# When an expert's second matrix gets its scale: after the first block of the first layer, or after the second

## The chip, the cores and the metric

The kernel runs on one core of one Trainium2 chip. The metric is the time of one execution in microseconds on the device; a kernel is run several times and the median is quoted. All times inside an execution are microseconds from its first instruction.

## The reference, cut to what matters

Three layers follow each other on 4 x 576 positions of width 512. The first is a retention layer with 8 heads. The second routes each position to one of 8 experts, and it is the one that the change touches:

```python
e = fresh_e if s == 0 or local_gate[b, s] < 0.5 else prev_e   # which expert
h = np.maximum(x[b, s] @ w1[e], 0.0)        # 512 -> 1024, "first layer"
out[b, s] = p[e] * (h @ w2[e])              # 1024 -> 512, "second layer"
```

The third layer is a Fourier mixing over positions and channels, a normalisation and a dense network of width 2048 with a residual (`u + relu(un @ w_ch1) @ w_ch2`). Everything is float32 in the reference.

## The kernel before, in words

**Split arithmetic.** Every float32 matrix is turned into two fp16 matrices, a high part `wh` and a residue `wl`, with one power-of-two scale for each matrix. A product is then three groups of fp16 matmuls (high x high, residue x high, high x residue). To get there a matrix of an expert goes through these steps (class `Weights`), in four pieces of 128 x 1024:

- `load`: SP issues the DMA of a piece into a tile `wst`.
- `absmax` (L234): ScalarE (ACT) sums magnitudes of a piece.
- `peak` (L243 to L255): three small VectorE (DVE) instructions reduce these to one exponent for each partition and write it on a diagonal, the tile `diag`.
- `spread` (L257 to L261): TensorE (PE) multiplies `diag` by a matrix of ones, so that every partition sees all exponents (L260), and DVE takes the maximum (`wg`, L261).
- `scale` (L263 to L269): two small DVE instructions make the scale `ws`.
- `split`: for each piece ACT writes the high part `wh` (`high`, L276), then DVE the residue `wl` (`low`, L281).

**The passes.** The function `moe` runs over eight lists of positions, `e` = 0 to 7; we call them passes 0 to 7. `CAPS` sets their widths: 128, 416, 320, 320, 320, 288, 288, and 128 (the rest of the last list is done later). A pass is a first layer and a second layer. The first layer is eight blocks; a block is 12 matmuls (L807) into one PSUM bank of the pool `p1`, which has four banks. Each block's result is taken out by `relu`: ACT writes the high part of `hid` (L823), DVE its residue (L825); only then is the bank free, and block 4 needs the bank of block 0, block 5 that of block 1, and so on. The second layer (L837) runs in tiles of 128 positions; ACT scales the result out (L849) and POOL scatters it to DRAM.

**Work beside the matmuls.** While a pass runs on the current expert's first matrix, its second matrix is split, and the next expert's matrices are measured and loaded. Besides, the third layer's weights, which arrive as 64-bit numbers (`raw`), are converted by DVE: `conv.first` (three instructions, L294 to L298) and `conv.second` (L303, L306), stored by SP, and measured by ACT (`conv.absmax`).

**What sets the order.** The order is written out by hand. The table `SLOTS` has one dict for the first layers (n = 2e) and one for the second layers (n = 2e + 1). A step's number k puts it behind block int(k) of a first layer (or behind the corresponding tile of a second layer); within one place lower numbers come first, and a negative number means the head of place 0. The function `halves` (L924) turns the table into a list for each place, and `moe` emits for each block `f`: the block's matmuls, the steps of place `f`, then the block's `relu`:

```python
products(nc, ps, *w.dst, xt, f)
for do in todo[f]:
    do()
```

So each engine gets its instructions in that order and works through them in that order; a step that waits holds up whatever stands behind it on its own engine. SP's queue holds, per pass, loads of `raw` and stores of converted weights, one big transposing DMA that brings the next pass's positions (`xt`, L1012), small ones, and eight loads of pieces. Another `spread` stands in the middle of each second layer's first tile (the argument `amid`), for the next expert's first matrix; it is not touched.

Of the kernel before, what the change touches and what calls it, by code (L numbers as in the profile page):

```python
# [863 lines left out]
class Late:  # L864
# [18 lines left out]
    def outputs(self, bank):  # L883
# [11 lines left out]
    dict(  # L895
        own=-1,
        second=0,
        spread=1,
        split=(1.1, 1.2, 2.1, 3.1),
        raw=1.2,  # L900
        store=1.3,
        fetch=1.4,
# [6 lines left out]
        spread=-1,  # L909
        first=(0, 4.2),  # L910
        factors=0.2,
        split=(0.5, 0.6, 1.5, 2.7),
# [1415 lines left out]
```

## Time and profile before

| what | value |
|---|---|
| time before, median of 3 runs | 814.44 us (811.02 to 817.1) |
| the profiled execution's own time | 811.84 us |
| its span, first to last instruction | 810.1 us |
| mean granted TensorE clock | 0.982 |
| PE busy | 740.1 us, 91% of the span |
| DVE busy | 593.3 us, 73% |
| ACT busy | 412.3 us, 51% |
| first layers of passes 2 to 7 | between 191.5 and 349.5 us |

The page is one profiled execution. "Busy" is a sum over the whole span; which engine limits a stretch has to be read in that stretch, from the waits. A row of the timeline gives the start, the length, the engine, the line, the operation, and in brackets how long the engine had been idle before and which instruction released it. In rows the names carry no buffer numbers: `ps` is a PSUM bank, `peak` the bank of a `spread`, `wst` a loaded piece, `d` a converted piece.

### The profile page before, as it was taken

The numbers are of one execution on the slowest core, as the hardware profiler recorded it, in microseconds if no ns is written. First come the engines' busy times: TensorE is split into PE (matmuls) and PEld (weight loads), VectorE is DVE, ScalarE is ACT, GpSimd is POOL, SyncE is SP. The second block draws the span as 40 slices with busy tenths as digits, with TensorE's granted clock in tenths as the row PEclk, the third lists the DMA queues.
The fourth block names the chain that finished last, engine by engine and source line by source line (L and its number), as shares of the span: only waits on it lengthen the run. The fifth ranks groups of instructions, "written<-read, shape, count | busy, mean of one in ns | idle before, by whom it ended". The sixth has DMA issues, their size and how long they took to land. (4 is left out here: it accounts for less than half of the span.)

```text
span 810.1 us, 17225 instructions
## 1 busy us (share of the span) xinstructions
PE 740.1 (91%) x6571; PEld 552.6 (68%) x6571; DVE 593.3 (73%) x1432; ACT 412.3 (51%) x829; POOL 129.9 (16%) x225
## 2 busy tenths in 40 slices
PE   7889888898889988889998999979899999999996
PEld 5778675555455555567644546868788888888885
DVE  3667886886879879757787976977958495737362
ACT  1445655675977977844764644605523361504040
POOL 3555543102012102111100002010010101010101
PEclk9999999899999999999999999999999999999998
DMA  9987439999998998843165457630270016100000
GB/s 287 357 292 263 162 112 291 236 312 367 263 378 289 262 352 296 265 135 110 46 213 185 154 188 199 198 75 15 92 217 2 27 53 170 53 34 21 27 2 27
DMA packets 91931, 142.29 MB, mean 176 GB/s; under 512 B 48117, under 2 KB 49018, under 8 KB 90815
## 3 DMA queue, kind: packets, MB, share of 16 engines
q1 hardware_dynamic: 87246, 126.78, 50.0%
q0 software_dynamic: 4592, 14.31, 4.6%
q8 instruction: 54, 0.88, 0.5%
q14 instruction: 39, 0.31, 0.1%
HBM read 97.55 MB, written 35.12 MB: 164 GB/s over the span
## 5 line engine op out<-in xcount | busy, mean ns | idle before, releaser
L1628 PE MATMUL g<-gxt,wh 128*128 128x256 f16 (+1 forms) x992 | 142.9, 284 | 3.0 <-DMA gxt<-un 2.9
L1942 PEld LDWEIGHTS <-hd 128*128 128x128 f16 x1176 | 114.2, 98 | 26.8 <-issue 7.2
L1628 PEld LDWEIGHTS <-wh 128*128 128x128 f16 x1056 | 103.0, 98 | 28.4 <-issue 6.7
L281 DVE SCALAR_TENSOR_TENSOR wl<-wst,ws,wh 128x1024 f16<-128x1024 f32 (+1 forms) x82 | 100.1, 1254 | 18.0 <-ACT wh L276 17.7
L276 ACT ACTIVATE wh<-wst,ws 128x1024 f16<-128x1024 f32 x80 | 88.6, 1139 | 39.1 <-DVE ws L269 39.1
L807 PE MATMUL ps<-xt,wh 128*128 128x320 f16 (+4 forms) x544 | 82.4, 290 | 21.3 <-DVE hid L825 13.8
L807 PEld LDWEIGHTS <-wh 128*128 128x128 f16 x640 | 58.9, 102 | 45.0 <-issue 27.3
L837 PE MATMUL ps<-wh,hid 128*128 128x512 f16 (+2 forms) x528 | 84.4, 302 | 0.8 <-ACT wh L276 0.8
L1942 PE MATMUL g<-wh,hd 128*128 128x256 f16 x448 | 78.3, 273 | 4.2 <-DVE u L1971 2.0
L1802 POOL DMA_INDIRECT out<-u,orow x18 | 19.3, 1075 | 388.8 <-DVE u L1971 291.6
L1628 PE MATMUL g<-gxt,wl 128*128 128x256 f16 (+1 forms) x496 | 79.5, 283 | 0.0
L837 PEld LDWEIGHTS <-hid 128*128 128x128 f16 (+2 forms) x792 | 46.4, 100 | 44.0 <-issue 3.6
L1913 DVE SCALAR_TENSOR_TENSOR s<-g,r 128x256 f32<-128x256 f32 x168 | 53.3, 374 | 30.3 <-ACT hd L1907 29.7
L234 ACT ACTIVATE wh<-wst 128x1024 bf16<-128x1024 f32 x66 | 69.1, 1048 | 3.8 <-DVE wst L306 3.8
L1971 DVE SCALAR_TENSOR_TENSOR u<-g,ffs,u 128x256 f32<-128x256 f32 (+1 forms) x63 | 34.1, 568 | 49.3 <-PE g L1942 48.7
L1906 ACT ACTIVATE r<-g 128x256 f32<-128x256 f32 x56 | 21.2, 378 | 91.4 <-PE g L1628 85.4
L851 POOL DMA_INDIRECT x<-y,mt x25 | 32.3, 1291 | 206.1 <-ACT y L849 159.4
L1886 ACT ACTIVATE hd<-s 128x640 f16<-128x640 f32 x56 | 41.3, 737 | 47.1 <-DVE s L1913 47.1
L1942 PE MATMUL g<-e,hd 128*128 128x256 f16 x504 | 60.0, 273 | 5.0 <-DVE u L1971 4.0
L1942 PE MATMUL g<-wl,hd 128*128 128x256 f16 x224 | 61.0, 272 | 0.0
L1628 PEld LDWEIGHTS <-wl 128*128 128x128 f16 x528 | 51.7, 98 | 11.4 <-issue 0.6
L837 PE MATMUL ps<-wl,hid 128*128 128x512 f16 (+2 forms) x264 | 56.3, 301 | 0.7 <-DVE wl L281 0.7
(302 smaller groups left out, 1304.6 us busy)
## 6 DMA issues: line engine op xcount, KB each, us to landing
wst<-in_moe_w SPq DMA_DIRECT2D x64, 512.0 KB
raw<-in_ch SPq DMA_DIRECT2D x14, 1024.0 KB
qk<-in_qkv SPq DMA_DIRECT2D x18, 512.0 KB
vk<-in_qkv SPq DMA_DIRECT2D x16, 512.0 KB
pair<-ch SPq DMA_DIRECT2D x32, 256.0 KB
ch<-d SPq DMA_DIRECT2D x14, 512.0 KB
wst<-ch SPq DMA_DIRECT2D x14, 512.0 KB
u<-u SPq DMA_DIRECT2D x9, 512.0 KB
```

The costliest lines, as they stand in the source:

```text
L234: self.nc.scalar.activation(out=x, in_=t, func=ACTF.Abs, accum_out=self.am[:, j : j + 1])
L276: self.nc.scalar.activation(out=self.dst[0][:, j, :], in_=self.pieces[j], func=ACTF.Copy, scale=self.by(j))
L281: self.nc.vector.scalar_tensor_tensor(out=l[:, j, c], in0=self.pieces[j][:, c], scalar=self.by(j), in1=h[:, j, c], op0=ALU.mult, op1=ALU.s ...
L807: nc.tensor.matmul(out=ps, lhsT=m[:, k, 128 * f : 128 * f + 128], rhs=xt[:, x + k, :], start=(k == 0 and i == 0), stop=(k == 3 and i == 2),)
L837: nc.tensor.matmul(out=ps[r * j : r * j + r, 0:d], lhsT=hid[x][:, f, 128 * t : 128 * t + r], rhs=m[:, 4 + f // 2, c : c + d], start=(f == ...
L851: nc.gpsimd.indirect_dma_start(out=x2[:, :].rearrange("t (k d) -> (t k) d", k=k), out_offset=bass.IndirectOffsetOnAxis(ap=mt, axis=0), in_ ...
L1628: nc.tensor.matmul(out=ps, lhsT=m[:, k + 4 * (f // 8), 128 * (f % 8) : 128 * (f % 8) + 128], rhs=xt[x][:, k, :], start=(k == 0 and i == 0) ...
L1886: nc.scalar.activation(out=hd[:, 0, 2:7], in_=s, func=ACTF.Copy, scale=C2 / 2)
L1906: nc.scalar.activation(out=r, in_=p[:, 1:3], func=ACTF.Relu)
L1913: V.scalar_tensor_tensor(out=d, in0=x, scalar=0.0, in1=y, op0=ALU.max, op1=op)
L1942: nc.tensor.matmul(out=ps, lhsT=hid[k][:, y, x, :], rhs=E[w][m][k], start=(k == 0 and m == y == 0), stop=(k == 7 and y == 1),)
L1971: V.scalar_tensor_tensor(out=y, in0=p, scalar=fs[:, c : c + 1], in1=y, op0=ALU.mult, op1=ALU.add)
```

## The change

Two numbers of the first-layer dict of `SLOTS`:

```diff
 SLOTS = [
     dict(
         own=-1,
         second=0,
-        spread=1,
-        split=(1.1, 1.2, 2.1, 3.1),
+        spread=-1,
+        split=(0.1, 1.1, 2.1, 3.1),
         raw=1.2,
```

`spread` and `scale` of the expert's second matrix stand behind block 0 instead of block 1, ahead of `conv.second`, which stays there; the first of the four splits moves from behind block 1 to behind block 0. This holds for the seven passes 1 to 7. The orders on SP and POOL are the same as before. On three engines the order of pass 4 shows it; the other passes read alike.

PE, between the blocks of pass 4's first layer (`ps_3535` is block 0's bank, `ps_3554` or `ps_3561` block 1's, `ps_3599` block 2's). Before:

```order
 L807 MATMUL ps_3554<-xt,wh_75 128x320
 L807 LDWEIGHTS wh_75
 L807 MATMUL ps_3554<-xt,wh_75 128x320
 L260 LDWEIGHTS onesb
 L260 MATMUL peak<-diag,onesb 128x128
 L807 LDWEIGHTS wh_75
 L807 MATMUL ps_3599<-xt,wh_75 128x320
```

And with the change:

```order
 L807 MATMUL ps_3535<-xt,wh_75 128x320
 L807 LDWEIGHTS wh_75
 L807 MATMUL ps_3535<-xt,wh_75 128x320
 L260 LDWEIGHTS onesb
 L260 MATMUL peak<-diag,onesb 128x128
 L807 LDWEIGHTS wh_75
 L807 MATMUL ps_3561<-xt,wh_75 128x320
```

The `spread` matmul moved ahead of the 12 matmuls of block 1.

DVE in the same stretch, from the diagonal of the second matrix to the residue of block 1. Before:

```order
 L255 TENSOR_SCALAR diag<-idn,wm 128x128
 L303 SCALAR_TENSOR_TENSOR d<-raw,d 128x1024
 L306 SCALAR_TENSOR_TENSOR d<-raw,d 128x1024
 L825 SCALAR_TENSOR_TENSOR hid<-ps_3535,hid 128x320
 L261 TENSOR_REDUCE wg<-peak 128x1
 L266 TENSOR_SCALAR wi<-wg 128x1
 L269 RECIPROCAL ws<-wi 128x1
 L281 SCALAR_TENSOR_TENSOR wl_76<-wst,ws,wh_75 128x1024 x2
 L825 SCALAR_TENSOR_TENSOR hid<-ps_3554,hid 128x320
```

And with the change:

```order
 L255 TENSOR_SCALAR diag<-idn,wm 128x128
 L261 TENSOR_REDUCE wg<-peak 128x1
 L266 TENSOR_SCALAR wi<-wg 128x1
 L269 RECIPROCAL ws<-wi 128x1
 L303 SCALAR_TENSOR_TENSOR d<-raw,d 128x1024
 L306 SCALAR_TENSOR_TENSOR d<-raw,d 128x1024
 L281 SCALAR_TENSOR_TENSOR wl_76<-wst,ws,wh_75 128x1024
 L825 SCALAR_TENSOR_TENSOR hid<-ps_3535,hid 128x320
 L281 SCALAR_TENSOR_TENSOR wl_76<-wst,ws,wh_75 128x1024
 L825 SCALAR_TENSOR_TENSOR hid<-ps_3561,hid 128x320
```

The three instructions of the scale moved ahead of `conv.second`, and block 0's residue now has one `low` ahead of it, block 1's residue one instead of two.

ACT in the same stretch (`ab` is the scratch of `conv.absmax`). Before:

```order
 L234 ACTIVATE ab,am<-d 128x1024
 L823 ACTIVATE hid<-ps_3535 128x320
 L276 ACTIVATE wh_75<-wst,ws 128x1024 x2
 L823 ACTIVATE hid<-ps_3554 128x320
 L276 ACTIVATE wh_75<-wst,ws 128x1024
```

And with the change:

```order
 L234 ACTIVATE ab,am<-d 128x1024
 L276 ACTIVATE wh_75<-wst,ws 128x1024
 L823 ACTIVATE hid<-ps_3535 128x320
 L276 ACTIVATE wh_75<-wst,ws 128x1024
 L823 ACTIVATE hid<-ps_3561 128x320
 L276 ACTIVATE wh_75<-wst,ws 128x1024
```

The first `high` now stands ahead of block 0's high part of `hid`.

## Rows read from the trace of the kernel before

**Rows 1.** The page's first part: engine, busy us (share of the span), instructions.

```profile
PE 740.1 (91%) x6571; PEld 552.6 (68%) x6571; DVE 593.3 (73%) x1432; ACT 412.3 (51%) x829; POOL 129.9 (16%) x225
```

**Rows 2.** What PE waited for, whole span: us in total, times, longest.

```profile
PE ps L807 <- DVE hid L825: 13.8, 10, 2.8
...
PE peak L260 <- DVE diag L255: 3.6, 3, 2.4
```

**Rows 3.** Windows, first layers of passes 2 to 7: length, engines' busy, PEclk, DMA share, GB/s.

```profile
191.50:210.40 18.90, 13.70 (x106) 9.44 (x99) 12.61 (x20) 11.40 (x20) 1.78 (x4) 1.00 1.03 406
223.60:239.20 15.60, 13.44 (x100) 9.46 (x99) 12.46 (x20) 11.49 (x20) 2.76 (x4) 1.00 1.03 393
252.40:268.00 15.60, 13.44 (x99) 9.45 (x98) 12.51 (x20) 11.45 (x19) 2.75 (x4) 1.00 1.02 384
281.30:297.50 16.20, 13.60 (x99) 10.19 (x98) 12.54 (x21) 12.07 (x22) 2.81 (x4) 0.89 1.03 386
309.50:326.00 16.50, 12.33 (x101) 9.39 (x98) 13.57 (x21) 11.98 (x22) 2.75 (x4) 1.00 1.02 378
338.00:349.50 11.50, 8.83 (x118) 6.67 (x110) 9.10 (x22) 8.30 (x18) 2.13 (x4) 1.00 0.75 282
```

**Rows 4.** Timeline of PE, pass 4 (start, length, instruction, idle before and releaser).

```profile
252.42 0.72 PE L807 MATMUL ps<-xt,wh 128*128 128x320 f16 x4
...
255.69 0.22 PE L260 MATMUL peak<-diag,onesb 128*128 128x128 bf16 x1
...
262.61 0.70 PE L807 MATMUL ps<-xt,wh 128*128 128x320 f16 x4 [1.81 <-DVE hid L825]
...
266.38 0.70 PE L807 MATMUL ps<-xt,wh 128*128 128x320 f16 x4 [0.35 <-DVE hid L825]
...
270.60 0.22 PE L260 MATMUL ps<-diag,onesb 128*128 128x128 bf16 x1
```

**Rows 5.** Timeline of DVE, pass 4.

```profile
254.74 0.29 DVE L255 TENSOR_SCALAR diag<-idn,wm 128x128 bf16<-128x128 f32 x1
254.94 1.22 DVE L303 SCALAR_TENSOR_TENSOR d<-raw,d 128x1024 int32<-128x1024 int32 x1
...
257.33 0.48 DVE L825 SCALAR_TENSOR_TENSOR hid<-ps,hid 128x320 f16<-128x320 f32 x1
257.74 0.28 DVE L261 TENSOR_REDUCE wg<-peak 128x1 f32<-128x128 f32 x1
...
258.24 0.16 DVE L269 RECIPROCAL ws<-wi 128x1 f32<-128x1 f32 x1
259.68 2.48 DVE L281 SCALAR_TENSOR_TENSOR wl<-wst,ws,wh 128x1024 f16<-128x1024 f32 x2 [1.28 <-ACT wh L276]
...
270.85 0.29 DVE L261 TENSOR_REDUCE wg<-ps 128x1 f32<-128x128 f32 x1 [0.43 <-PE ps L260]
```

**Rows 6.** Timeline of ACT, pass 4.

```profile
258.50 2.19 ACT L276 ACTIVATE wh<-wst,ws 128x1024 f16<-128x1024 f32 x2 [3.80 <-DVE ws L269]
260.59 0.41 ACT L823 ACTIVATE hid<-ps 128x320 f16<-128x320 f32 x1
```

**Rows 7.** Timeline of PE: pass 5's second layer, then pass 6.

```profile
300.11 0.22 PE L260 MATMUL ps<-diag,onesb 128*128 128x128 bf16 x1
...
313.42 0.22 PE L260 MATMUL peak<-diag,onesb 128*128 128x128 bf16 x1 [0.82 <-DVE diag L255]
```

**Rows 8.** Timeline of DVE and then of PE, pass 2.

```profile
194.62 0.69 DVE L294 TENSOR_SCALAR d<-raw 128x1024 int32<-128x1024 int32 x1 [6.42 <-DMA raw<-in_ch]
...
197.40 0.23 PE L260 MATMUL peak<-diag,onesb 128*128 128x128 bf16 x1 [2.45 <-DVE diag L255]
```

**Rows 9.** Windows in pass 5: its wait in the first layer, and what follows.

```profile
288.80:292.30 3.50, 0.90 (x9) 0.68 (x8) 3.50 (x4) 3.50 (x7) 0.00 (x0) 1.00 1.01 400
292.30:295.70 3.40, 3.40 (x17) 2.15 (x15) 2.39 (x4) 3.40 (x7) 0.00 (x0) 0.50 1.05 399
```

**Rows 10.** Window behind the transposing DMA for pass 6.

```profile
303.50:306.50 3.00, 3.00 (x16) 1.35 (x14) 3.00 (x4) 3.00 (x4) 1.29 (x1) 1.00 0.07 1
```

## The prediction

> **What bounds the kernel now.** I read the page first, then what PE waited for, then the passes one by one. The page has PE busy for 91% of the span and DVE for 73% [rows 1], so a gain has to come out of PE's gaps. The list of PE's waits shows which gaps this change can touch: in the first layers PE waited 13.8 us, ten times, for the residue of `hid`, and 3.6 us, three times, for the diagonal of a peak [rows 2]. The windows of the first layers show how these are spread: eight blocks of 320 columns take 15.6 us in passes 3 and 4 with PE busy for 13.4 of it, and the 288-wide passes 5 and 6 take longer, 16.2 and 16.5, although they have less to do [rows 3].
>
> The timeline of pass 4 says why. Two blocks lie between 252.42 and the `spread` at 255.69, so a block is 1.64 us. Later PE stands 1.81 us ahead of block 5 and 0.35 us ahead of block 7, each time until DVE has written a residue [rows 4], which frees a bank of `p1`. DVE is late there since the two splits come in one lump: it finishes the scale at 258.40, waits 1.28 us for ACT's first `high`, does two `low` in 2.48 us, and only then block 1's residue [rows 5]; ACT has its own lump of two `high`, 2.19 us, ahead of block 1's `hid` [rows 6].
>
> The Trainium skill, Perfetto Trace Analysis, section Optimization Strategy, says that the same gap repeated on an engine that should be saturated "can mean there isn't enough SBUF/PSUM for the next tile to be allocated". The trace agrees that a bank is what PE waits for; by that rule alone the four banks stay four and the time stays too, which is the first rival.
>
> **The new wait.** `spread` will stand where block 0 ends, at 252.42 + 1.64 = 254.06, but DVE finishes `diag` at 254.74 + 0.29 = 255.03 [rows 5]. So PE now waits 1.0 us in pass 4 where it waited for nothing, and blocks 1 to 7 stand behind that wait. When the diagonal is ready is set by DVE alone: from the previous `spread`, in the middle of a second layer, DVE works without a gap through the scale, a conversion, four `low` and another conversion and a half. Pass 6 shows the length of that chain where PE really waited for it: 313.42 - 300.11 = 13.3 us [rows 7]. Nothing in it is changed.
>
> **The rest of a first layer, counted from the `spread` S.** The durations are those of pass 4.
> - DVE takes the maximum 0.25 us after the matmul (270.60 to 270.85) and has the scale 0.66 us after that (257.74 to 258.40): S + 0.9. `conv.second` follows, 2.4 us (254.94 to 257.33) [rows 5]. It is 1.05 us later behind the diagonal than before; SP's next load of `raw` and its store wait for it, and I come to them under the second rival.
> - ACT starts the first `high` 0.1 us behind the scale, S + 1.0, and is free for block 0's `hid` at S + 2.1, half of its lump of 2.19 [rows 6].
> - DVE does the first `low` at S + 3.3 (1.2 us) and block 0's residue from S + 4.4 to S + 4.9. Then `low` and residue alternate, 1.2 + 0.4 = 1.6 us a pair: residues of blocks 1, 2 and 3 end near S + 6.5, 8.1 and 9.7.
> - PE runs blocks 1, 2, 3 from S + 0.06 to S + 4.97. Block 4 needs residue 0 (S + 4.9), block 5 residue 1 (PE is there at 6.6, it is ready at 6.5), block 6 residue 2 (8.2 against 8.1), block 7 residue 3 (9.9 against 9.7). So 320-wide blocks just run through: block 7 ends at S + 11.5. With 288 columns a block is 1.47 us, PE catches up with the residues, waits some 0.5 us ahead of block 4, and block 7 ends near S + 11.1.
>
> **The sum, pass by pass.** A new first layer is block 0, the wait for the diagonal, and the stretch from S.
> - Passes 3 and 4: 1.64 + 1.0 + 11.5 = 14.2 against 15.6 [rows 3]: -1.4 each. In pass 3 everything that counts is shifted by what went before, PE and DVE alike.
> - Pass 5: the second layer before it is that of a 320-wide pass; its first layer starts 281.3 - 270.6 = 10.7 us after the middle `spread` [rows 3, 4], so the wait is 13.3 - 10.7 - 1.47 = 1.15. 1.47 + 1.15 + 11.1 = 13.7 against 16.2: -2.4. Of this some 0.9 is clock: PE's wait of 2.6 us there was followed by 3.4 us at 0.50 of the clock, the 1.2 GHz level [rows 9], and no wait of that length is left in pass 5.
> - Pass 6: its first layer starts 309.5 - 300.1 = 9.4 us after the middle `spread` [rows 3, 7], so the wait grows to 13.3 - 9.4 - 1.47 = 2.4 (it was 0.82 after two blocks [rows 7]). 1.47 + 2.4 + 11.1 = 15.0 against 16.5: -1.5.
> - Pass 7: 128-wide blocks, no `conv.second`; PE is paced by the splits themselves, which begin earlier by one residue on DVE and one `hid` on ACT. Bounds: 0, and pass 4's -1.4. I take the middle, -0.7, as half of pass 4's causes are there.
> - Pass 2: DVE had idled 6.42 us until a DMA of `raw` landed at 194.6, the diagonal came late, and PE already waited 2.45 us behind two blocks [rows 8]. The landing stays, for the DMA share is 1.03 in that window and SP's order is the same. So S stays at 197.40 and PE now waits 197.40 - 191.5 - 1.64 = 4.2 us. Block 7 would end at S + 11.5 = 208.9 against 210.4: -1.4 at full clock. But 4.2 us is longer than the wait that brought the clock to 0.50 [rows 9]; 3.4 us at half clock cost up to 1.7, which makes +0.3. Some of that stretch will lie inside the wait; I take 0, bounds -1.4 and +0.3.
> - Pass 1: the diagonal is early, since DVE had time after the last conversion, and PE's blocks of 416 columns leave room. 0.
>
> Sum: 0 - 1.4 - 1.4 - 2.4 - 1.5 - 0.7 = -7.4 us. Against the profiled execution, 811.84 us, that is 804.4. What follows pass 7 hangs on its last outputs and shifts along. The median of the runs, 814.44, lies 2.6 above the profiled one; I put the sum on the median: **807.0 us**.
>
> **The rivals.**
> - *The wait only moves.* PE stops for the diagonal instead of the residue, and the banks come no sooner. For it: the new waits add up to 4.2 + 1.0 + 1.0 + 1.15 + 2.4. Against it: behind S the residues follow 1.6 us apart, as fast as PE's blocks. Gain 0 to 2, time about 813.5. Chance 0.1.
> - *The DMA chain becomes the bound.* The DMA engines are at a share of 1.02 to 1.03 in every first layer but the last [rows 3], and rest only behind the transposing DMA (0.07 from 303.5 to 306.5 [rows 10]) while SP works through small ones, on its own pace. Positions for pass 6 are therefore in at about 303.5, 6.0 us ahead of their use at 309.5. I have taken 5.2 out by then, so it fits, with 0.8 left; a full -1.4 in pass 2 would already meet it, and so -8 in all is about the most that can be had. If the later loads of `raw` and stores (1.05 us a pass) push the transposes back as well, 2 to 4 us of the slack go: gain 3 to 5, time about 810.5. Against this: when those are issued, the queue still holds some microseconds of earlier transfers. Chance 0.14.
> - *The clock falls in every pass*, the case that ends slower. Each `spread` now makes PE wait; if each wait is followed by 3.4 us at half clock [rows 9], six passes lose up to 1.7 each, 10.2. Without any such stretch before or after, the gain is 7.4 + 1.4 (pass 2) - 0.9 (the one of pass 5) = 7.9; 10.2 - 7.9 - 0.9 = +1.4: about 816. It decides at the length of wait that makes the clock fall: 2.6 did in pass 5, the 2.45 of pass 2 did not (that window is at 1.00 throughout [rows 3]), and four of the six new waits are 1.2 or less. Chance 0.08. The Trainium skill, TensorE: Matmul & The Clock Gate, section HAM oscillation, tells of a kernel whose TensorE waited for data in each K tile and ran each tile at the half rate. Passes 3, 4 and 6 here, with waits of up to 2.8 us [rows 2] at a clock of 1.00 [rows 3], do not show that.
> - *More than forecast.* Other executions before had more half-clock stretches than the profiled one (the median is 2.6 slower), and the change removes the waits that cause them in passes 3 to 5. Gain 8.2 to 10.5, time about 805. Chance 0.23.
>
> The forecast itself, a gain of 5 to 8.1, has 0.45.
>
> **How the numbers follow.** About 1% of this kernel's time, 8.1 us, is what a measurement can tell from no change; the runs before spread from 811.0 to 817.1. Faster by over 1% needs the last rival and some luck of the runs: 0.26. Slower by over 1% needs the clock rival at its full price and more: 0.04. The rest, 0.70, lies within 1%, most of it on the fast side. The range takes in pass 2 at full clock and the fast rival below, and the DMA rival and most of the moving wait above: 803 to 813.
>
> **What will show it.** Windows of the first layers: 14.2 us in passes 3 and 4, 13.7 and 15.0 in 5 and 6. PE's list of waits: residue down from 13.8 us to under 3, diagonal up from 3.6 to about 10, of which 4.2 in pass 2 and 2.4 in pass 6. The clock: 0.50 for about 3.4 us in pass 2, none in pass 5. If PE waits for `xt` at the head of passes 5 to 7, the DMA rival is at work; if the residue still ends PE's waits ahead of blocks 5 and 7, my replay of DVE's queue is wrong; if 0.50 appears behind the short waits of passes 3 and 4, it is the clock.

## The result, and the profile after

| | before | changed |
|---|---|---|
| median of 5 runs each | 813.08 us (811.02 to 817.1) | 803.05 us (802.46 to 806.81) |
| ratio | | 0.9886, 95% interval 0.9855 to 0.9917 |
| the profiled execution: time, span | 811.84, 810.1 us | 806.81, 805.0 us |
| pass 1's first block to the end of the expert stage | 213.25 us | 204.50 us |

The change makes the kernel 1.1% faster, 10.0 us against the 7.4 that were forecast. The expert stage ends with the first matmul of the third layer's network (L1593), which comes 8.27 us earlier now. These rows of PE's timeline give pass 1's first block and that matmul, before (first two) and now (start, length, instruction).

```profile
155.68 1.50 PE L807 MATMUL ps<-xt,wh 128*128 128x416 f16 x4 [2.31 <-DMA xt<-xs]
...
368.93 0.59 PE L1593 MATMUL bank<-wh 128*128 128x512 f16 x2
...
156.16 0.86 PE L807 MATMUL ps<-xt,wh 128*128 128x416 f16 x4 [2.24 <-DMA xt<-xs]
...
360.66 0.59 PE L1593 MATMUL bank<-wh 128*128 128x512 f16 x2
```

The page's first part of the changed kernel answers to [rows 1] (engine, busy us, share of the span, instructions):

```profile
PE 738.7 (92%) x6571; PEld 552.4 (69%) x6571; DVE 591.2 (73%) x1432; ACT 411.8 (51%) x829; POOL 130.0 (16%) x225
```

Busy times have hardly moved; the gain is in the gaps. What PE waited for, over the whole span (us in total, times, longest), beside [rows 2]:

```profile
PE ps L807 <- DMA xt<-xs: 7.5, 3, 2.8
...
PE peak L260 <- DVE diag L255: 5.1, 4, 2.2
...
PE ps L260 <- DVE diag L255: 1.6, 1, 1.6
PE ps L807 <- DVE hid L825: 1.3, 2, 1.0
...
PE peak L260 <- DVE wm L251: 0.9, 1, 0.9
```

The waits for a residue have all but gone, from 13.8 us to 1.3. The waits for the diagonal come to 7.6 us in three rows: the last is pass 4's, put down to the instruction before the diagonal, and the 1.6 is a `spread` in the middle of pass 1's second layer. The row at the top is new in part: the wait for positions ahead of pass 6.

Windows of the first and second layers of passes 2 to 6 in turn, with the columns of [rows 3]; the first layers answer to these:

```profile
192.30:208.20 15.90, 13.48 (x99) 9.38 (x98) 12.54 (x21) 11.85 (x22) 1.89 (x4) 1.00 1.02 404
208.20:221.50 13.30, 13.30 (x100) 7.25 (x98) 11.98 (x22) 11.25 (x18) 1.67 (x2) 1.00 0.98 230
221.50:235.60 14.10, 13.25 (x100) 9.41 (x99) 12.32 (x21) 11.97 (x22) 2.75 (x4) 1.00 1.00 373
235.60:248.90 13.30, 13.30 (x100) 7.23 (x98) 11.97 (x22) 11.24 (x18) 1.68 (x2) 1.00 0.96 265
248.90:263.00 14.10, 13.25 (x100) 9.41 (x99) 12.32 (x21) 11.98 (x22) 2.75 (x4) 1.00 0.99 356
263.00:276.20 13.20, 13.20 (x99) 7.19 (x96) 11.88 (x22) 11.22 (x18) 1.73 (x2) 1.00 0.95 276
276.20:290.00 13.80, 12.43 (x99) 9.43 (x98) 12.21 (x21) 11.54 (x21) 2.80 (x4) 1.00 0.96 315
290.00:304.90 14.90, 12.06 (x148) 6.08 (x146) 13.45 (x24) 12.66 (x22) 3.10 (x4) 1.00 0.97 304
304.90:318.40 13.50, 13.50 (x98) 10.24 (x98) 10.56 (x18) 10.13 (x19) 1.34 (x3) 0.87 0.91 302
```

The second layers of passes 3 to 5 in the kernel before, same columns:

```profile
239.20:252.40 13.20, 13.20 (x98) 7.17 (x96) 11.97 (x22) 11.76 (x21) 1.68 (x2) 1.00 0.88 223
268.00:281.30 13.30, 13.30 (x100) 7.25 (x98) 12.03 (x22) 11.79 (x21) 1.73 (x2) 1.00 0.82 191
297.50:309.50 12.00, 12.00 (x148) 6.02 (x146) 10.42 (x20) 9.87 (x16) 1.68 (x2) 1.00 0.80 190
```

The first layers of passes 3 and 4 take 14.1 us where they took 15.6. The second to last column, the DMA share, is the one to keep: in the second layers it rose from between 0.80 and 0.88 to between 0.95 and 0.97, so that the DMA engines have little idle time left. Most of the gain did not come out of that idle time, though: over the whole stretch from 195 to 300 us the share is 0.99 before and 1.00 now, at 320 and 324 GB/s. SP's timeline has the transposing DMAs for passes 5 and 6, before (first two rows) and now (start of the issue, how long it held SP's queue):

```profile
261.31 11.34 SPq L1012 DMA_TRANSPOSE xt<-xs  x1
...
291.67 10.32 SPq L1012 DMA_TRANSPOSE xt<-xs  x1
...
260.57 11.49 SPq L1012 DMA_TRANSPOSE xt<-xs  x1
...
290.64 10.13 SPq L1012 DMA_TRANSPOSE xt<-xs  x1
```

They were issued 0.7 and 1.0 us earlier than before, while PE ended pass 5's first layer 7.5 us earlier. What the faster passes used up is above all the lead that the transfers had on PE.

The Trainium skill, DMA: Bandwidth & Descriptors, section Latency and other measured facts, gives a transposing DMA with a non-contiguous middle dimension an effective 261 GB/s, and the contiguous case 350 to 400. The trace agrees in so far as a stretch with a transposing DMA moves less: the second layer of pass 2, which holds most of one, has a share of 0.98 at 230 GB/s, the first layer before it 1.02 at 404. No run here has the two kinds of transposing DMA to compare. So "full" has to be read in the share, not in GB/s.

### The profile page after: what moved, and what is told of

Read it like the earlier page. It is cut to its first block, busy times and chain, and to the rows that moved or that the text cites. A ratio compares the mean times of both kernels' runs of the same rounds, so it can differ in the third digit from the quotient of the medians.

```text
span 805.0 us, 17230 instructions
## 1 busy us (share of the span) xinstructions
PE 738.7 (92%) x6571; PEld 552.4 (69%) x6571; DVE 591.2 (73%) x1432; ACT 411.8 (51%) x829; POOL 130.0 (16%) x225
## 5 line engine op out<-in xcount | busy, mean ns | idle before, releaser
L281 DVE SCALAR_TENSOR_TENSOR wl<-wst,ws,wh 128x1024 f16<-128x1024 f32 (+1 forms) x82 | 100.6, 1252 | 11.3 <-ACT wh L276 11.1
L807 PE MATMUL ps<-xt,wh 128*128 128x320 f16 (+4 forms) x544 | 80.0, 285 | 12.1 <-DMA xt<-xs 7.5
```

The source lines that it names most:

```text
L281: self.nc.vector.scalar_tensor_tensor(out=l[:, j, c], in0=self.pieces[j][:, c], scalar=self.by(j), in1=h[:, j, c], op0=ALU.mult, op1=ALU.s ...
L807: nc.tensor.matmul(out=ps, lhsT=m[:, k, 128 * f : 128 * f + 128], rhs=xt[:, x + k, :], start=(k == 0 and i == 0), stop=(k == 3 and i == 2),)
```

## The experiments

All were timed in five rounds against the kernel before, in three groups of four, each group on one chip; "the stage" is the stretch from pass 1's first block to L1593 in the profile (the same matmul stands at L1597 in the kernels with less DMA).

| kernel | median, us | ratio to before (95%) | the stage, us |
|---|---|---|---|
| changed, again | 800.33 | 0.9862 (0.9837 to 0.9888) | 204.65 |
| changed, third time | 803.14 | 0.9902 (0.9873 to 0.9931) | 202.85 |
| before, again | 811.15 | 0.9994 (0.9977 to 1.0012) | 212.74 |
| spread alone | 800.93 | 0.986 (0.9835 to 0.9885) | 202.84 |
| scale behind the conversion | 809.36 | 0.9969 (0.9948 to 0.9989) | 210.24 |
| early peak | 802.67 | 0.9894 (0.9867 to 0.9921) | 206.15 |
| early fetch | 805.54 | 0.9929 (0.9907 to 0.9952) | 208.14 |
| both early | 805.72 | 0.9914 (0.9886 to 0.9942) | 207.14 |
| before, early fetch | 811.42 | 0.9992 (0.9974 to 1.0011) | 212.98 |
| early peak, less DMA | 799.9 | 0.9867 (0.9836 to 0.9899) | 201.38 |
| changed, less DMA | 802.26 | 0.9884 (0.9856 to 0.9913) | 202.09 |
| before, less DMA | 810.87 | 0.9994 (0.9972 to 1.0015) | 214.90 |

### How large the gain is

The changed kernel and the kernel before, each as it stands.

> The changed kernel once more, beside the others on one chip. Queue-order theory (the gain is the scale standing ahead of the conversion and of block 1): the first layers of passes 3 and 4 end 11.5 us after their spread, as in the first profile, and the time is 8 to 11 us below the kernel before. Clock theory (a good part of the 10 us is where the half-clock stretches fall): the expert passes are again some 8.3 us shorter, but the number and the places of the stretches at 0.5 differ from the first profile, and the span with them by 2 to 4 us.

> The changed kernel a third time, timed against the kernel before. The stage alone is 8.1 to 8.8 us shorter in the profiles, which is a ratio of 0.989 to 0.990; the two timings gave 0.9886 and 0.9862. If the stage is all, the three together come to about 0.988 with 0.989 inside the interval of this one; if there is a gain beyond the stage, this one is again below 0.988 and its interval leaves 0.990 out.

> The kernel before once more, as a kernel of its own. Ratio 1.000 with an interval of about 0.003 to each side. Its profile is a second sample: if the 10 us measured for the change come from the expert stage alone, this profile shows that stage 8 to 10 us longer than the change's (213 to 215 us) and the rest the same within 3 us; if the rest of the kernel differs by more than that from profile to profile, the part of the 10 us beyond the stage's 8.3 is where in the stretches behind it the clock happens to halve.

The three timings of the change give 10.0, 11.3 and 8.1 us (each median against that of before on its chip), 9.8 on average. The profiles of the change have a stage of 202.85 to 204.65, the two of before 212.74 and 213.25: 9.0 us on average. So the stage explains the gain to within a microsecond. Outside the stage the profiles of both kernels scatter alike: 441 to 444 us behind it.

### Which of the two edits does it

Spread alone: `spread` and `scale` as in the change, the splits as before.

```diff
-        split=(0.1, 1.1, 2.1, 3.1),
+        split=(1.1, 1.2, 2.1, 3.1),
```

> The spread ahead of block 1, but the splits where they were before (two behind block 1). Queue-order theory: the scale ahead of the conversion is what counts, and the split's place nothing; block 0's residue comes some 1.1 us earlier than in the changed kernel, block 1's at the same 6.5 us behind the spread; passes 3 and 4 end 11.5 us behind their spread, pass 5 a few tenths sooner; time within 1 us of the changed kernel. Rival (the lump of two splits is what held the banks, so taking it apart is the gain): PE again waits near 2 us ahead of block 5 in every pass, and 5 us or more of the gain are lost.

Measured: 800.93 us, and a stage of 202.84, as short as the shortest of the change. From `spread` to the end of pass 4's first layer it takes 11.46 us against 11.48. The place of the first split is worth nothing that can be seen.

Scale behind the conversion: PE's order as in the change, but DVE takes the maximum and makes the scale behind `conv.second`, so that against the kernel before PE's `spread` and the first split are earlier, and the scale stays where it was on DVE, behind the conversion.

```diff
-        spread=-1,
+        spread=0.05,
```

> As the changed kernel, but the spread and the scale stand behind conv.second in the same place (0.05 instead of -1): PE has the same order, DVE does its two conversion instructions first. Queue-order theory: the scale is ready some 2 us later behind the diagonal (3.0 instead of 0.9), PE waits 1 to 2 us ahead of block 4 and the first layer ends 12.3 to 12.6 us behind the spread instead of 11.5; about 0.9 us a pass, 4 to 5 us of the gain are lost. Rival (it is PE's order that counts: the spread ahead of block 1): time as the changed kernel.

Timeline of PE, then of DVE, pass 4 of this kernel:

```profile
252.71 0.22 PE L260 MATMUL peak<-diag,onesb 128*128 128x128 bf16 x1 [0.84 <-DVE diag L255]
258.65 0.70 PE L807 MATMUL ps<-xt,wh 128*128 128x320 f16 x4 [0.84 <-DVE hid L825]
263.94 0.70 PE L807 MATMUL ps<-xt,wh 128*128 128x320 f16 x4 [0.24 <-DVE hid L825]
```

```profile
252.57 1.22 DVE L303 SCALAR_TENSOR_TENSOR d<-raw,d 128x1024 int32<-128x1024 int32 x1
...
254.96 0.28 DVE L261 TENSOR_REDUCE wg<-peak 128x1 f32<-128x128 f32 x1
...
256.91 1.28 DVE L281 SCALAR_TENSOR_TENSOR wl<-wst,ws,wh 128x1024 f16<-128x1024 f32 x1 [1.28 <-ACT wh L276]
```

With the conversion first, DVE reads the peak 2.25 us behind the matmul, where the change reads it 0.25 behind, and then stands idle 1.28 us for ACT's first `high`, which the conversion had covered. PE pays 0.84 and 0.24, and from `spread` to the end of the layer it takes 12.86 us in place of 11.48, a loss of 1.4 where 0.9 was expected. The stage is 6.2 us longer than the mean of the change's three, against 4 to 5 expected. So of the 9.0 us that the stage gains on average, 2.8 come with PE's earlier `spread` and the earlier first split, and the other 6 only when the maximum and the scale go ahead of the conversion on DVE.

### What bounds the kernel now

Early peak: `conv.first` stands later, so that DVE reaches the diagonal some 2 us sooner.

```diff
-        first=(0, 4.2),
+        first=(0, 7.35),
```

> As the changed kernel, but in the second layers DVE makes the peak's diagonal ahead of the three instructions of the next conversion instead of behind them (first at 7.35 instead of 4.2), so the diagonal is ready 2.1 us earlier. If DVE's chain alone set the passes, PE's waits for the diagonal in passes 3 to 6 (0.85 to 1.1 us) go and the expert passes end 3 to 4 us earlier. DMA theory (positions of pass 6 come no sooner): passes 3 to 5 get shorter by about 1 us each, the wait for xt ahead of pass 6 grows from 2.8 us to 5 or 6 us, and the end of the expert passes moves by less than 1 us.

Timeline of PE in passes 4 and 6 of this kernel:

```profile
247.10 0.22 PE L260 MATMUL peak<-diag,onesb 128*128 128x128 bf16 x1
...
252.68 0.70 PE L807 MATMUL ps<-xt,wh 128*128 128x320 f16 x4 [0.47 <-DVE hid L825]
...
303.73 1.12 PE L807 MATMUL ps<-xt,wh 128*128 128x288 f16 x4 [5.85 <-DMA xt<-xs]
```

The diagonal is no longer waited for, and each of passes 3 to 5 is 0.4 us shorter, as a residue wait comes back behind the conversion. But all of it and more turns up ahead of pass 6: the wait for positions grew from 2.84 to 5.85 us. The stage, 206.15, was expected within 1 us of the change's and is 2.1 us above the mean of its three; the positions themselves were in 150.4 us behind pass 1's first block, against 148.7 and 148.8 in the change's first two profiles, and why is not shown.

Early fetch: SP issues the transposing DMA ahead of the load of `raw` and the store, in the changed kernel, in the one with the early peak, and in the kernel before.

```diff
-        fetch=1.4,
+        fetch=1.15,
```

> The changed kernel, with the transposing DMA for the next pass's positions issued by SP ahead of the pass's load of raw and its store of a converted piece, not behind them. Theory (the order of SP's queue sets when the positions come, and at pass 6 that has become the bound): the raw load and the store of a pass took about 3.7 us of the queue in the changed kernel, so the positions come that much earlier; PE's wait for xt ahead of pass 6 (2.84 and 2.94 us in the two profiles of the change) is gone, the wait for the diagonal there becomes 1 to 2 us instead, and the stretch from pass 1 to the end of the expert stage is 1 to 2 us shorter than the 204.5 us of the change; the time about 799. Rival (the amount of bytes bounds the stretch, at a DMA share of 1.02 whatever the order): the wait only changes its name, from xt to a piece or to raw through the diagonal, the stretch stays within 0.5 us of 204.5. Third: the raw load, now later, makes the first conversion and with it the diagonal late in pass 2 and after, and the stretch is 1 to 3 us longer.

> As the kernel with the early transposing DMA, and besides the first third of the conversion stands about one residue split later in the second layer, so that DVE reaches the peak and its diagonal 2.1 us earlier. Theory (with the positions early enough, the chain on DVE from one spread to the next diagonal is the only bound left, and taking 2.1 us out of it shortens each of passes 3 to 6 by what it did before with the diagonal alone, 0.4 us each, and pass 6 by its wait for the diagonal): 2 to 3.5 us less than the 204.5 us of the change from pass 1 to the end of the stage; time about 798, below both kernels. Rival (DMA bytes bound it): the stretch stays within 0.5 us of 204.5 and PE waits for xt ahead of pass 6 as long as with the early peak alone (5.85 us) or for the pieces.

> The kernel before, with only the transposing DMA moved ahead of the load of raw and of the store. Theory (before, the positions for pass 6 had about 6 us to spare, so that their transfer bounded nothing): 0, within 0.5 us of the 213.25 us from pass 1 to the end of the expert stage, or up to 1 us longer where raw now lands later (pass 2). Rival (the positions' transfer was part of the bound before the change already): 2 us or more shorter.

In the kernel before it is worth nothing, as expected. In the changed one the wait for `xt` is gone, yet the stage is 4.1 us longer than the mean of the change's three. Timeline of DVE, and then of PE, in pass 6 of the early fetch:

```profile
305.49 0.69 DVE L294 TENSOR_SCALAR d<-raw 128x1024 int32<-128x1024 int32 x1 [1.77 <-DMA ch<-d]
...
307.93 0.29 DVE L255 TENSOR_SCALAR diag<-idn,wm 128x128 bf16<-128x128 f32 x1
```

```profile
308.27 0.26 PE L260 MATMUL peak<-diag,onesb 128*128 128x128 bf16 x1 [4.17 <-DVE diag L255]
```

The store, now issued at 297.93 behind the transposing DMA, landed 7.6 us later, and `conv.first` needs the tile that it empties. DVE stood still 1.77 us, the diagonal was late, and PE waited 4.17 us for it. The third theory had the direction; it named the load of `raw`, and the row of pass 6 names the store. In pass 2, which the theory named, DVE waited 5.30 us for `raw` and PE 2.95 us for the diagonal, and a stretch at 0.50 of the clock followed that none of the change's profiles has there. The kernel with both changes was expected to be the best and is not: its DVE meets the store in the first layer, and PE waits 2.33 and 2.93 us for residues in passes 4 and 5 (DVE's rows, then PE's):

```profile
250.11 0.73 DVE L294 TENSOR_SCALAR d<-raw 128x1024 int32<-128x1024 int32 x1 [1.74 <-DMA ch<-d]
...
278.82 0.86 DVE L294 TENSOR_SCALAR d<-raw 128x1024 int32<-128x1024 int32 x1 [1.55 <-DMA ch<-d]
```

```profile
256.91 0.70 PE L807 MATMUL ps<-xt,wh 128*128 128x320 f16 x4 [2.33 <-DVE hid L825]
...
285.72 1.12 PE L807 MATMUL ps<-xt,wh 128*128 128x288 f16 x4 [2.93 <-DVE hid L825]
```

Reordering the queue moved the wait from one user of the DMA engines to another. What remained was to take bytes away (the lines of the diff that matter):

```diff
+        self.old = {}
 ...
     def load(self, j):
-        r = self.pool.tile([128, 1024, 2], I32, tag="raw", name="raw", bufs=2)
+        if 8 <= j <= 13:
+            self.raw[j] = self.old[j % 2]
+            return
+        r = self.old[j % 2] = self.pool.tile([128, 1024, 2], I32, tag="raw", name="raw", bufs=2)
```

Six loads of `raw` are left out, and the conversions work on the piece that is already in the tile.

> The kernel with the early peak, and the six loads of raw that passes 3 to 5 issue (one in each first and one in each second layer) are left out; the conversions then work on the piece that is already in the tile, so that the converted weights are not the right ones, while every engine has the same instructions. Theory (the DMA chain has become the bound of passes 3 to 6, whatever its order): PE's wait for xt ahead of pass 6, 5.85 us in the early-peak kernel, goes or falls below 1, and the stretch from pass 1 to the end of the expert stage falls from 206.15 to 200 to 202, below the 204.5 us of the change. Rival (the positions come late by something other than the load of the DMA engines, as the transposing DMA's own 10 us behind a buffer that PE frees): the wait for xt stays at 4 us or more, the stretch at 205 or more.

> The changed kernel with the same six loads of raw left out. Theory: PE's wait for xt ahead of pass 6 (2.8 to 2.9 us) becomes the wait for the diagonal that was forecast there, 2.4 us or a little less behind block 0; the stretch from pass 1 to the end of the stage is 1 to 2.5 us shorter than the change's 204.5. Rival: the wait for xt stays, 204.5.

> The kernel before with the same six loads left out, as the control. If DMA did not bound passes 3 to 6 before the change, the stretch from pass 1 to the end of the stage stays at 212.7 to 213.3 us; if it did, it falls by 2 us or more.

PE at pass 6 of the changed kernel with less DMA, and the window of pass 5's second layer of the early peak with less DMA (columns as above):

```profile
306.01 0.22 PE L260 MATMUL peak<-diag,onesb 128*128 128x128 bf16 x1 [2.27 <-DVE diag L255]
```

```profile
287.80:299.80 12.00, 12.00 (x148) 6.05 (x146) 10.66 (x21) 10.17 (x17) 1.65 (x2) 1.00 0.74 218
```

Without the six loads (1024 KB each) the wait for `xt` at pass 6 is gone from both kernels. The changed one shows there the wait for the diagonal that the prediction had worked out, 2.27 against 2.4 us, and its stage is 2.4 us under the 204.5 of the expectation and 1.9 under the mean of the three. The early peak, which gained nothing before, now has a stage of 201.38, 4.8 less than with the loads. The control, the kernel before, did not gain: 214.90 against 212.74 and 213.25, and the timing says 0.9994. That its stage was 1.7 us longer I had not expected. About 1.1 us of it is clock: its windows from 204.3 to 207.7 us and from 320.3 to 323.7 are at 0.50 and 0.51, and from `spread` to the end of the first layer passes 2 and 6 take 14.09 and 13.54 us, where the first profile of before, at 1.00 in both layers, has 12.93 and 12.63; pass 5, which has the stretch at 0.50 there [rows 9], is 0.95 us shorter.

So the DMA chain did not bound passes 3 to 6 before the change, and after it PE reaches pass 6 before the positions do. Leaving out the loads takes away their places in SP's queue as well as their bytes; that the bytes count shows in the transposing DMA for pass 6, which is the same in both kernels and held SP's queue for 10.13 us in the change and for 5.83 with less DMA. The timings are too coarse for this step: 0.9884 and 0.9867 lie within the 0.9862 to 0.9902 of the change's own three, so it rests on the profiles. No version tried here that computes everything is faster than the change beyond the scatter.

## Why the prediction was right, point by point

The forecast was 807.0 us, measured was 803.05. Of the 4.0 us between, 1.4 are the median of before, on which the sum was put (814.44 then, 813.08 with two runs more), 0.9 are the stage (8.27 at its end against 7.4), and the other 1.7 I put down to the scatter of executions. That 803.05 lies in the range of 803 to 813 is luck, by 0.05 us: the other two medians of the change are 803.14 and 800.33. The mean gain of the three timings, 9.8 us, is the size of the rival "more than forecast" (chance 0.23), but not by its reason, fewer half-clock stretches: the mean granted clock is 0.982 in both first profiles. In the stage pass 2 gave 2.1 us more than forecast and pass 6 1.3 less, so the sum came out close by two errors that partly cancel. What was right is the mechanism in passes 3 to 5.

How much earlier PE reaches each place than before, in the two first profiles:

| place | forecast | measured | step |
|---|---|---|---|
| end of pass 2's first layer | 0 | 2.1 | -2.1 against 0 |
| pass 3's | 1.4 | 3.6 | -1.5 against -1.4 |
| pass 4's | 2.8 | 5.0 | -1.5 against -1.4 |
| pass 5's | 5.2 | 7.5 | -2.5 against -2.4 |
| pass 6's | 6.7 | 7.7 | -0.2 against -1.5 |
| end of the stage | 7.4 | 8.3 | -0.6 against -0.7 |

**The new wait and the replay behind `spread`: right.** PE's timeline of pass 4, to be read beside [rows 4]:

```profile
248.85 0.72 PE L807 MATMUL ps<-xt,wh 128*128 128x320 f16 x4
...
251.50 0.22 PE L260 MATMUL peak<-diag,onesb 128*128 128x128 bf16 x1 [0.85 <-DVE wm L251]
...
262.98 0.59 PE L837 MATMUL ps<-wh,hid 128*128 128x512 f16 x2
...
265.57 0.22 PE L260 MATMUL ps<-diag,onesb 128*128 128x128 bf16 x1
```

The `spread` stands 2.65 us behind block 0's start, of which 1.0 was forecast as wait, and blocks 1 to 7 then run to the second layer in 11.48 us without a gap; 11.5 was the replay. In pass 5 the same stretch is 11.08 us for a forecast of 11.1. DVE and ACT of pass 4, beside [rows 5, 6]:

```profile
251.16 0.29 DVE L255 TENSOR_SCALAR diag<-idn,wm 128x128 bf16<-128x128 f32 x1
251.75 0.29 DVE L261 TENSOR_REDUCE wg<-peak 128x1 f32<-128x128 f32 x1 [0.31 <-issue]
...
254.73 1.28 DVE L281 SCALAR_TENSOR_TENSOR wl<-wst,ws,wh 128x1024 f16<-128x1024 f32 x1
255.93 0.48 DVE L825 SCALAR_TENSOR_TENSOR hid<-ps,hid 128x320 f16<-128x320 f32 x1
256.33 1.28 DVE L281 SCALAR_TENSOR_TENSOR wl<-wst,ws,wh 128x1024 f16<-128x1024 f32 x1
257.52 0.48 DVE L825 SCALAR_TENSOR_TENSOR hid<-ps,hid 128x320 f16<-128x320 f32 x1
```

```profile
252.53 1.15 ACT L276 ACTIVATE wh<-wst,ws 128x1024 f16<-128x1024 f32 x1 [2.06 <-DVE ws L269]
253.58 0.42 ACT L823 ACTIVATE hid<-ps 128x320 f16<-128x320 f32 x1
```

The first residue begins at S + 4.4, as worked out, and `low` and residue alternate 1.6 us apart. The four banks are the same four, and the gaps that named them are gone: the rule of the Trainium skill (Perfetto Trace Analysis, section Optimization Strategy), that a repeated gap can mean too little PSUM, gave the place of the wait and not its cause, which was DVE's order.

**Pass 2: the term that was mis-sized.** Rows of DVE and PE beside [rows 8]:

```profile
193.85 0.72 DVE L294 TENSOR_SCALAR d<-raw 128x1024 int32<-128x1024 int32 x1 [5.22 <-DMA raw<-in_ch]
```

```profile
196.71 0.23 PE L260 MATMUL peak<-diag,onesb 128*128 128x128 bf16 x1 [2.17 <-DVE diag L255]
```

I had held `spread` at 197.40, with a wait of 4.2 us and a stretch at half clock behind it. It came 0.7 us sooner: the load of `raw` that DVE waited for was issued at 184.09 us (184.08 before) and landed 0.8 us earlier. The four loads of pieces behind it in SP's queue were issued 1.3 us later than before (188.15 against 186.89); whether that is why is not shown. PE reached it later, too, since pass 1's `spread` in its second layer waited 1.57 us. The wait was 2.17, the clock stayed at 1.00, and the 1.4 us of the replay came in full. This -2.1 was outside my bounds of -1.4 and +0.3. It is no accident of one profile: behind pass 1's first block, pass 2's first layer ends after 51.5 to 52.1 us in the three profiles of the change, and after 54.48 and 54.65 in the two of before.

**Pass 6: the rival that came true in part.** I gave 0.14 to the DMA chain as the bound and "about -8" as the most that can be had. The first block of pass 6 stood here:

```profile
304.89 0.65 PE L807 MATMUL ps<-xt,wh 128*128 128x288 f16 x4 [2.84 <-DMA xt<-xs]
```

By the end of pass 5 7.5 us had been taken out, more than the slack of 6.0, and the positions took back 2.84, 1.3 more than the excess, so they also came that much later than before. The other two profiles of the change wait 2.94 us there, and 1.58 (a wait that the third puts down to ACT). So the wait of 2.4 us for the diagonal, the term that I had for pass 6, did not come in the change's first two profiles; it showed only with less DMA. The half clock that followed (0.87 in pass 6's window) cost little: block 0 to the end of the layer took 13.49 us with it and without a further wait, and 13.37 in the third profile, which has no half clock there but waits 0.66 and 0.30 us. The mechanism was priced as a rival and left out of pass 6's term, because pass 2 was to fill none of the slack. That reordering the queue gains nothing here is shown by the kernels with the early fetch; that fewer bytes end the wait, by those with less DMA.

**The clock.** It did not fall behind the short waits of passes 3 to 5, as forecast, and pass 5, at 0.89 before [rows 3], is at 1.00. In pass 2 it did not fall either, which was not forecast. The prediction had it that the length of the wait decides; the last section has rows that speak against that.

## What to carry to other kernels

Where a wait ends with a bank that DVE frees, look for a lump in DVE's own order before looking for more banks: one instruction that starts a chain over three engines, placed so that other work covers the chain's answer time, was worth more here than the matmul's place. When a gap is closed, read first how far ahead of their use the transfers land, and the DMA share of the stretches beside it: the time that was won here came out of that lead, 6.0 us at pass 6, and out of what idle time the DMA engines had, and when both are used up the next closed gap comes back as a wait for a transfer. The one reordering of SP's queue that was tried only changed which transfer that was.

## What the runs showed of the hardware

The length of a wait alone does not tell whether the clock falls to 0.50 behind it. Waits of 2.84, 2.93, 4.17 and 5.85 us (pass 6 of the change, pass 5 of both early, pass 6 of the early fetch and of the early peak) went with 3.4 us at 0.50 that began within 0.7 us of their end; waits of 2.27 us (pass 6 of the change with less DMA), 2.17 and 1.57 (passes 2 and 1 of the change) went without. A shorter wait of 2.14 us, for the diagonal in the middle of pass 1 in the second profile of the change, ended at 175.12 us, and the window from 176.1 to 179.5 is at 0.50. Before the change a wait of 2.6 us was followed by such a stretch [rows 9], and those of up to 2.8 us [rows 2] in pass 6 were not.
